# Windowed attention in two layers: when each stack of queries and keys is loaded, and which PSUM bank a late projection uses

## The chip, the cores and the metric

The kernel runs on one core of a Trainium2 chip. The metric is the device time of one execution in microseconds, as the median over runs. The core has five engines that run side by side, each through its own list of instructions in order: TensorE (PE; its weight loads are shown as PEld), VectorE (DVE), ScalarE (ACT), GpSimd (POOL) and SyncE (SP). SP, ACT and POOL can also issue DMAs; here most of them stand in SP's list. Semaphores make an instruction wait for others.

## The reference

The input is a sequence of 2048 tokens of 576 numbers. Four steps are added to it in turn: attention, a filter in the frequency domain, attention, the filter. Both attentions use the same weights, and so do both filters. The attention has 32 heads of 18 numbers, and a query sees itself and the 255 keys before it:

```
qkv = (layernorm(x) @ wqkv)  ->  q, k, v with H = 32 heads of Dh = 18
scores = einsum("bhqd,bhkd->bhqk", q, k) * Dh ** -0.5
mask = (idx[:, None] - idx[None, :] >= 0) & (idx[:, None] - idx[None, :] < 256)
p = softmax(where(mask, scores, -1e9))
x = x + einsum("bhqk,bhkd->bhqd", p, v) @ wo
x = x + irfft2(rfft2(layernorm(x)) * (w_r + 1j * w_i))
```

## The kernel before

One Python program writes all instructions, and the order in which it writes them is each engine's order. It builds two attention layers (`layer_a`), each followed by a filter layer (`layer_b`). The change is in `layer_a`, so it acts twice.

**Quads, chunks, blocks.** The 32 heads are worked on in 8 quads of four heads; a quad is two halves of partitions (hp) by two pairs. The 2048 tokens are 16 tiles of 128, and four tiles are a chunk. So a block, x = 16 n + i, is tile i of quad n, and there are 128 of them. (n, c) below is chunk c of quad n.

**Projections.** q and k of all heads are 1152 rows, computed as 9 groups of 128 rows by 4 chunks: `proj(i, c)`, 14 matmuls of 512 columns each into one PSUM bank (line 1112). The result is split into a rounded part, which ScalarE copies out (line 1124, CAST), and a remainder, which VectorE subtracts (line 1127). Then a DMA stores both to `qk_d` in DRAM (line 1129). The subtraction and the store are kept in the list `ended` and written when `remainders()` is called, so they come later in the engines' lists than the copy. Groups i = 0, 1 are projected first, groups 2 to 8 in pieces between the attention's own work; their 392 matmuls are the list `pj`. Staging tiles of groups 0 to 2 share room with the tiles of exponentials (tag "P", six of them).

**Stacks.** `stack_load(n, c)` (line 1135) brings one chunk of a quad's q and k from `qk_d` into one of two sets of tiles, `qs` and `ks`, quads n and n + 2 using the same set. It is twelve DMAs of 72 KB, six for q and then six for k; nearly all stand in SP's list. A chunk of quad n reads rows of two groups of projections: group n + 1 is the later one for n = 2 to 7.

**Scores, maxima, exponentials, sums.** For each block and head there is a score tile (`score_max`: matmul at line 1169, masked row maximum on VectorE at line 1171) and, ten blocks later (LEAD = 10), an exponent tile (`exps`: matmul at line 1206, exponential on ScalarE at line 1207, masks on GpSimd). Between the two, `m_rows(n, c)` transposes the maxima of a chunk on TensorE (line 1182), ScalarE copies them with the sign turned (line 1184), and four DMAs write them as a row of `qs` (line 1189, qs<-mt), from which the exponent matmul subtracts them. The exponent tile of block x reads tiles x to x + 2 of q, so it needs the row of the chunk that holds tile x + 2. `part(x, half)` adds the values weighted by the exponentials into the PSUM tile U (line 1226), and `norm` transposes the finished sums (line 1240), divides, and stores them (line 1251).

**Order.** `opening()` runs score tiles of blocks 0 to 9 with the first 70 matmuls of `pj`, which are projections (2,0) to (2,3) and (3,0). `bursts()` then covers blocks 0 to 117 in 158 bursts, k = 0 to 157. Each burst has three exponent tiles and three score tiles, that is three quarters of a block, and behind them a few matmuls of `pj`, or sums, or small tasks. `loads(x)` is called where a burst starts block x. How many matmuls of `pj` a burst gets follows from `ends`, the last burst in which each projection may run: (3,1) is spread over bursts 0 to 3, (3,2) over the next ones up to burst 8, and so on. Bursts listed in `values` (4, 7, 9, ...) have sums instead. Blocks 118 to 127 follow in a shorter loop.

**Near the end** SP's list also gets, from block 104 on, the output weights in two pieces (`out.room`, line 734), five constants (`out.const`, line 748, the first at block 107) and input tiles (`out.load_x`, line 759).

**PSUM.** It has eight banks. Tag "S" has three for score tiles, "E" three for exponent tiles (and, early, some projections and transposes), "pj" one for projections, and "U" one. In the opening every fourth score tile of a block uses "U"; from then on U holds the sums. Of each 32 rows of U only 19 are written by the sums, but the whole bank is copied and transposed, so it is set to zero once (line 1421).

Of the kernel before, what the change touches and what calls it, by code (L numbers as in the profile page):

```python
# [8 lines left out]
F32 = mybir.dt.float32  # L9
# [9 lines left out]
NT = 16  # L19
# [659 lines left out]
def k_steps():  # L679
    s = []  # L680
    for kt in range(4):
        s += [(kt, "h", kt), (kt, "h", 4 + kt)]
    for kt in range(4):
        s += [(kt, "l", kt)]
    s += [(4, "h", 8), (4, "l", 8)]
    return s
# [178 lines left out]
def layer_a(tc, ident, eps, bp, src, dst, wqk_d, wv_d, wo_d, dc_d, gc_d, dram, copy, wvs, second, spectral, share):  # L865

    nc = tc.nc
    V, A, T, P = nc.vector, nc.scalar, nc.tensor, nc.gpsimd
# [11 lines left out]
    def tokens(x, c):  # L880

        return x.rearrange("r (n p) -> r n p", n=NT)[:, :, 32 * c:32 * c + 32]
    if True:
        room = []

        def xT(k, c):

            xh, xl = room
            return xl[:, k - 4, c] if 4 <= k < 8 else xh[:, min(k, 4), c]
# [8 lines left out]
        def w_split(i):  # L898
            raw = wraws[i]
            h = bp.tile([128, 5, 128], F32R, tag="wqh", name=f"wqh{i}", bufs=2)  # L900
            l = bp.tile([128, 5, 128], F32R, tag="wql", name=f"wql{i}", bufs=2)
            wt[i] = (h, l)
            split_w(nc, raw, h, l, V if i == 2 else P)
            if i + 2 < 9:
                w_load(i + 2)
# [170 lines left out]
        with ExitStack() as c2:  # L1076
            wp = c2.enter_context(tc.tile_pool(name="a2", bufs=2))
            pp = Banks(tc, c2, "a2p", ("S", "pj"))
# [7 lines left out]
            for j in range(2):  # L1086
                q = wp.tile([128, 2, S], F32R, name=f"qs{j}", bufs=1)
                k = wp.tile([128, 2, S], F32R, name=f"ks{j}", bufs=1)
# [5 lines left out]
            def remainders():  # L1094
                while ended:
                    ended.pop(0)()

            def proj(i, c, bank=0):

                box = {}  # L1100
                ks = k_steps()
                cs = slice(c * 512, c * 512 + 512)

                def mm(s, k):
                    wk, p, xk = k
                    if s == 7 and c == 2 and 0 < i < 8:
                        w_split(i + 1)
                    if s == 0:
                        box["ps"] = pp.tile([128, 512], F32, tag="E" if bank else "pj", name=f"pj{i}_{c}", bufs=3 if bank else 1)
                    w = wt[i][0] if p == "h" else wt[i][1]  # L1110
                    x = tokens(xT(xk, slice(0, S)), c) if second else xT(xk, cs)
                    T.matmul(box["ps"].rearrange("r (n p) -> r n p", n=NT) if second else box["ps"], w[:, wk], x, start=s == 0, stop=s == len(ks) - 1)  # L1112
                    if s == len(ks) - 1:
                        if 4 * i + c < 12:

                            sg = wp.tile([128, 4, 384], F32, tag="P", name=f"sg{i}_{c}", bufs=6)
                            sg = sg.rearrange("r a b -> r (a b)")[:, 0:1024].rearrange("r (a t) -> r a t", a=2).bitcast(F32R)
                        else:
                            sg = wp.tile([128, 2, 512], F32R, tag="sg", name=f"sg{i}_{c}", bufs=2)
                        by, rest = box["ps"], sg  # L1120
                        if second:
                            by = by.rearrange("r (n p) -> r p n", n=NT)
                            rest = sg.rearrange("r a (p n) -> r a p n", n=NT)
                        A.copy(rest[:, 0], by)  # L1124

                        def remainder():
                            V.tensor_sub(rest[:, 1], by, rest[:, 0].bitcast(F32))  # L1127

                            (nc.scalar if i < 2 else nc.sync).dma_start(qk_d[:, 128 * i:128 * i + 128, cs].rearrange("a r t -> r a t").bitcast(F32), sg.bitcast(F32))
                        ended.append(remainder)  # L1130
                return [lambda s=s, k=k: mm(s, k) for s, k in enumerate(ks)]

            vts = {}
# [23 lines left out]
            def score_max(x, pair, hp):  # L1157
# [9 lines left out]
                four = x < LEAD and pair == hp == 1  # L1167
                ps = pp.tile([128, 512], F32, tag="U" if four else "S", name=f"S{x}_{pair}_{hp}", bufs=1 if four else 3)
                T.matmul(ps[:, 0:N], q[b:b + 63, pair, i * 128:i * 128 + 128], k[b:b + 63, pair, lo:hi], start=True, stop=True)  # L1169
# [47 lines left out]
            def part(x, half):  # L1217
# [6 lines left out]
                for h in range(4):  # L1224
                    if j >= 0:
                        T.matmul(U[32 * h:32 * h + 19, (q0 % 4) * 128:(q0 % 4) * 128 + 128 * (q1 - q0)], vts[n][:, j, h],  # L1226
                                 pt[n, j][:, h, (q0 - j) * 128:(q1 - j) * 128],
                                 start=j == max(e - 1, 0), stop=j == i or (i == e and j == i - 2), skip_group_check=True)
                if half and i % 4 == 3:
                    us[n, i // 4] = u = wp.tile([128, 512], F32, tag="us", name=f"us{n}_{i}", bufs=1)  # L1230
                    (V.tensor_copy if x >= MIX - 2 else A.copy)(u, U)  # L1231

# [29 lines left out]
                    stack_load(0, k // 2 - 1)  # L1262
            NX = NQ * NT
            LEAD = 10
            pj = [f for i in range(2, 9) for c in range(4) for f in proj(i, c, c % 2 if i == 2 else c == 0 and i == 3)]
            done, due = 0, []

            MIX = 118
# [1 line left out]
            def loads(t):  # L1270
                if t + LEAD in (0, 2):
                    stack_load(0, 2 + (t + LEAD) // 2)
                if t in (-4, 4, 8, 12):
                    stack_load(1, max(t, 0) // 4)
                n, c = divmod(t + 20, NT)
                if c % 4 == 0 and 1 < n < NQ:
                    stack_load(n, c // 4)
                if t + LEAD == 5:
                    v_load(0)
                if t + 12 in range(NT, NX, NT):  # L1280
                    v_load((t + 12) // NT)
# [28 lines left out]
            def bursts():  # L1310
# [2 lines left out]
                ss = [(x + LEAD, pair, 1 - hp) for x, pair, hp in es]  # L1313
                parts = [(x, half) for x in range(MIX - 2) for half in range(2) if x % NT]
                values = {(4 * x + 7) // 3 + 2 for x in range(0, MIX - 2, 2)}
                ends = [3] + [max(k - 1 for k in values if k - 1 <= 4 + 134 * (i + 1) // 22) for i in range(22)]
                unit = {k: i for i, end in enumerate(ends) for k in range(ends[i - 1] + 1 if i else 0, end + 1)}
                at = 70
                for k in range(-(-len(es) // 3)):
                    e, c = es[3 * k:3 * k + 3], ss[3 * k:3 * k + 3]  # L1320
# [28 lines left out]
                    n = 0  # L1349
                    if k in unit and k not in values:  # L1350
# [3 lines left out]
                        n = -(-rest // gaps)  # L1354
                        if gaps > 1 and any(f is norm for f, *a in tasks):
                            n = min(5, n + 1, rest - 2 * (gaps - 1))
# [60 lines left out]
            for f in opening():  # L1417
                f()
                done += 1
            U = pp.tile([128, 512], F32, tag="U", name="U", bufs=1)  # L1420
            V.memset(U, 0.0)
            for f in bursts():
                f()
                done += 1
# [18 lines left out]
            def bank(tag, name):  # L1443
                return pp.tile([128, 512], F32, tag=tag, name=name, bufs=1 if tag == "pj" else 3)

            out.early(0, [bank(k, f"ops0_{k}") for k in ("pj", "S")], slice(0, 4))
            tpz = [bank("E", f"tpz{k}") for k in range(3)] + [U]

# [16 lines left out]
            for u in range(3):  # L1465
                out.split_last(u, tp[:, 128 * u:128 * u + 128])
            out.turn(3, U, A)
            out.late(0)
# [50 lines left out]
```

## Time and profile before

| | us |
|---|---|
| median of 3 runs | 1366.31 (1366.28 to 1366.6) |
| the profiled execution | 1367.9 |
| its span, first to last instruction | 1366.2 |
| mean granted TensorE clock | 0.997 of full speed |
| attention bursts, first layer | from 127.6 |
| attention bursts, second layer | from 825.1 |

The profile of one execution is read through views. The page gives each engine's busy time. The waits name, for each line, what its engine waited for: total us, times, longest. The timeline lists instructions by engine: start, duration, engine, line, operation, output <- inputs, count, and in square brackets how long the engine stood idle and what released it. "SPq" is SP's own list of DMA issues; the duration there is that of issuing, not of the transfer. The windows give, for a stretch of time, its length and then the busy us of PE, PEld, DVE, ACT and POOL with the number of instructions, the granted TensorE clock, the share of the DMA engines, and GB/s. Bursts are found in the timeline by their first score tile. A PE that is busy need not be at its peak, and matmuls overlap, so the distance between starts tells more than durations.

### The profile page before, as it was taken

What the parts mean: (1) busy time and instruction counts of PE and PEld (TensorE: products, weight loads), DVE (VectorE), ACT (ScalarE), POOL (GpSimd) and SP (SyncE); (2) the same over time, 40 slices, a digit from 0 to 9 for tenths busy, and PEclk for the clock granted to TensorE, in tenths of its full rate; (3) what the DMA queues carried; (4) which work ended last, traced back from release to release, by engine and by line L of the source; (5) the groups of instructions that cost most, each with busy time, mean ns of one, the idle gap of its engine ahead of it and who ended that gap; (6) DMA issues with size and microseconds to landing.
All of it is one profiled execution on the core that took longest, in us unless ns stands there. A gap on an engine that the chain in (4) does not pass through costs nothing.

```text
span 1366.2 us, 33609 instructions
## 1 busy us (share of the span) xinstructions
PE 1335.8 (98%) x11351; PEld 997.2 (73%) x11351; DVE 900.5 (66%) x3060; ACT 780.0 (57%) x1966; POOL 644.0 (47%) x1154
## 2 busy tenths in 40 slices
PE   9999999999999999999999999999999999999998
PEld 8986666666665699975999965566666655898587
DVE  5418777877778376666663157777777785576745
ACT  5522777777778544542455316677777778464223
POOL 3257545555546533476221394455455458213721
PEclk9999999999999999999999999999999999999999
DMA  6756665655446457778773467555555555597875
GB/s 204 208 164 194 207 190 166 188 166 160 150 145 180 129 154 249 223 237 266 253 243 73 114 194 224 160 170 162 153 158 153 157 157 168 143 359 253 301 234 173
DMA packets 202425, 259.11 MB, mean 190 GB/s; under 512 B 104599, under 2 KB 109975, under 8 KB 201743
## 3 DMA queue, kind: packets, MB, share of 16 engines
q1 hardware_dynamic: 191551, 235.72, 57.0%
q10 hardware_dynamic: 7648, 14.96, 3.1%
q0 software_dynamic: 3056, 6.28, 1.8%
q8 instruction: 92, 1.51, 0.5%
q14 instruction: 78, 0.64, 0.2%
HBM read 156.11 MB, written 101.01 MB: 188 GB/s over the span
## 4 chain that ended last, share of the span: by engine, by line
PE 87%; DMA 4%; DVE 3%; ACT 2%; issue 2%; SPq 1%; POOL 0%; ACTq 0%; DVEq 0%; POOLq 0%
PE pj L1112 19%; PE S L1169 12%; PE U L1226 12%; PE vps L1005 8%; PE ops L800 7%; PE E L1206 6%; PE po L257 3%; PE pq L517 2%; PE tpo L1240 2%; PE pf L257 2%; PE p L496 2%; PE pi L591 2%; PE pz L295 2%; DMA ofree<-yd 1%; PE tpm L1182 1%
## 5 line engine op out<-in xcount | busy, mean ns | idle before, releaser
L1171 DVE CUSTOM_DVE_ANT_0 jk<-S,mask 128x384 bf16<-128x384 f32 (+2 forms) x1024 | 490.7, 529 | 113.5 <-PE E L1206 60.3
L1207 ACT ACTIVATE P<-E 128x384 f32<-128x384 f32 (+2 forms) x1024 | 409.1, 476 | 128.0 <-PE E L1206 99.2
L1209 POOL TENSOR_SCALAR_AFFINE_SELECT P<-P 128x512 f32<-128x512 f32 x256 | 162.6, 635 | 278.2 <-ACT P L1207 257.3
L1169 PE MATMUL S<-ks,qs 63*128 63x384 f32 (+2 forms) x1024 | 269.1, 371 | 1.0 <-DMA qs<-qk_d 0.4
L1206 PE MATMUL E<-qs,ks 64*128 64x384 f32 (+2 forms) x1024 | 222.4, 372 | 6.4 <-DMA qs<-mt 3.7
L1169 PEld LDWEIGHTS S<-ks,qs 63*128 63x128 f32 x1024 | 140.7, 185 | 105.4 <-DVE m L1171 72.4
L1226 PE MATMUL U<-P,vq 128*19 128x128 f32 (+1 forms) x3840 | 188.3, 329 | 0.6 <-DVE us L1231 0.2
L1112 PE MATMUL pj<-xh,wqh 128*128 128x512 f32 x360 | 156.2, 434 | 1.7 <-DVE sg L1127 1.3
L1226 PEld LDWEIGHTS U<-P,vq 128*19 128x19 f32 x3840 | 96.0, 98 | 77.7 <-issue 25.0
L1212 POOL TENSOR_SCALAR_AFFINE_SELECT P<-P 128x512 f32<-128x512 f32 x224 | 142.3, 635 | 0.0
L1206 PEld LDWEIGHTS E<-qs,ks 64*128 64x128 f32 x1024 | 113.7, 185 | 21.3 <-ACT P L1207 9.7
L1112 PE MATMUL pj<-xh,wql 128*128 128x512 f32 x360 | 124.4, 418 | 0.0
L1112 PE MATMUL pj<-xl,wqh 128*128 128x512 f32 x288 | 122.3, 425 | 0.0
L800 PE MATMUL ops<-oroom 128*128 128x290 f32 (+1 forms) x812 | 115.4, 298 | 0.4 <-DVE ofree L846 0.2
L800 PEld LDWEIGHTS ops<-oroom 128*128 128x128 f32 x812 | 110.2, 189 | 1.1 <-DVE ofree L823 0.7
L1112 PEld LDWEIGHTS pj<-xh,wqh 128*128 128x128 f32 x360 | 67.8, 188 | 32.5 <-issue 10.5
L1171 DVE DVE_READ_ACCUMULATOR2_ANT m<- 128x1 f32 x1024 | 85.3, 83 | 0.0
L1127 DVE TENSOR_TENSOR sg<-pj,sg 128x512 fp32r<-128x512 f32 x72 | 49.5, 687 | 52.5 <-ACT sg L1124 52.5
L1124 ACT CAST sg<-pj 128x512 fp32r<-128x512 f32 x72 | 42.2, 586 | 69.2 <-PE pj L1112 54.2
L1112 PEld LDWEIGHTS pj<-xh,wql 128*128 128x128 f32 x360 | 64.3, 189 | 20.3 <-issue 10.7
L1005 PE MATMUL vps<-wvh,xh 128*128 128x288 f32 x320 | 71.4, 304 | 0.0
L1112 PEld LDWEIGHTS pj<-xl,wqh 128*128 128x128 f32 x288 | 54.3, 189 | 18.3 <-issue 11.6
(599 smaller groups left out, 2257.5 us busy)
## 6 DMA issues: line engine op xcount, KB each, us to landing
qk_d<-sg SPq DMA_DIRECT2D x56, 512.0 KB
qs<-qk_d SPq DMA_DIRECT2D x384, 72.0 KB
ks<-qk_d SPq DMA_DIRECT2D x348, 72.0 KB
v_d<-vt SPq DMA_DIRECT2D x32, 304.0 KB
vq<-v_d SPq DMA_DIRECT2D x16, 608.0 KB
wt<-in_w SPq DMA_DIRECT2D x16, 580.0 KB
ofree<-x SPq DMA_DIRECT2D x16, 580.0 KB
x<-ofree SPq DMA_DIRECT2D x32, 290.0 KB
```

The source lines that it names most:

```text
L257: T.matmul(ps[:, c, 0:NF], tail[r] if si == 4 else hl_(si), dcs[b // 2][r, b % 2], start=mi == si == 0, stop=si == 4)
L800: self.nc.tensor.matmul(self.ps[u][n][:, 0:self.n], x, self.w[p][:, (2 * wk + n) * self.n:(2 * wk + n + 1) * self.n], start=first and i == ...
L1005: T.matmul(ps[:, n, 0:288], xT(xk, c), w[:, wk, n * 288:(n + 1) * 288], start=i == 0, stop=i == len(ks) - 1)
L1112: T.matmul(box["ps"].rearrange("r (n p) -> r n p", n=NT) if second else box["ps"], w[:, wk], x, start=s == 0, stop=s == len(ks) - 1)
L1127: V.tensor_sub(rest[:, 1], by, rest[:, 0].bitcast(F32))
L1169: T.matmul(ps[:, 0:N], q[b:b + 63, pair, i * 128:i * 128 + 128], k[b:b + 63, pair, lo:hi], start=True, stop=True)
L1171: V.tensor_tensor_reduce(out=jk[:, 0:N], in0=ps[:, 0:N], in1=mask[:, 384 - N:384], scale=1.0, scalar=-3e38, op0=ALU.add, op1=ALU.max, accu ...
L1206: T.matmul(ps[:, 0:nq], k[b:b + 64, pair, j * 128:j * 128 + 128], q[b:b + 64, pair, j * 128:j * 128 + nq], start=True, stop=True)
L1207: A.activation(p[:, hl_, 0:nq], ps[:, 0:nq], AF.Exp, scale=SC)
L1209: P.affine_select(out=p[:, :, 0:128], in_=p[:, :, 0:128], pattern=[[0, 4], [1, 128]], compare_op=ALU.is_ge, fill=0.0, base=0, channel_mult ...
L1212: P.affine_select(out=p[:, :, 256:384], in_=p[:, :, 256:384], pattern=[[0, 4], [-1, 128]], compare_op=ALU.is_gt, fill=0.0, base=0, channel ...
L1226: T.matmul(U[32 * h:32 * h + 19, (q0 % 4) * 128:(q0 % 4) * 128 + 128 * (q1 - q0)], vts[n][:, j, h], pt[n, j][:, h, (q0 - j) * 128:(q1 - j) ...
```

## The change

Five lines are edited.

- The loads of quads 2 to 7 are asked for four blocks later: (n, c) at block 16 n - 16 + 4 c instead of 16 n - 20 + 4 c. Quads 0 and 1 keep their own places.
- Projection (3,0), the last of the opening, uses the bank "pj" instead of one of the "E" banks.
- Projection (3,1), the first of the bursts, uses the tile U itself instead of the bank "pj"; it writes every row and column of it, and the line that sets U to zero is removed.
- `remainders()` is called once more between opening and bursts, so that the subtraction and store of (3,0) come ahead of burst 0's score tiles instead of behind them.
- (3,1) has to end with burst 2 instead of burst 3. Its 14 matmuls are then 5, 5, 4 in bursts 0 to 2 (before: 4, 4, 3, 3 in bursts 0 to 3), and those of (3,2) are 4, 4, 3, 3 in bursts 3, 5, 6, 8 (before: 5, 5, 4 in bursts 5, 6, 8). From burst 9 on nothing changes in that list.

```diff
@@ proj
                     if s == 0:
-                        box["ps"] = pp.tile([128, 512], F32, tag="E" if bank else "pj", name=f"pj{i}_{c}", bufs=3 if bank else 1)
+                        box["ps"] = U if bank == 2 else pp.tile([128, 512], F32, tag="E" if bank else "pj", name=f"pj{i}_{c}", bufs=3 if bank else 1)
@@ the list pj
-            pj = [f for i in range(2, 9) for c in range(4) for f in proj(i, c, c % 2 if i == 2 else c == 0 and i == 3)]
+            pj = [f for i in range(2, 9) for c in range(4) for f in proj(i, c, c % 2 if i == 2 else 2 if (i, c) == (3, 1) else 0)]
@@ loads
                 if t in (-4, 4, 8, 12):
                     stack_load(1, max(t, 0) // 4)
-                n, c = divmod(t + 20, NT)
+                n, c = divmod(t + 16, NT)
                 if c % 4 == 0 and 1 < n < NQ:
                     stack_load(n, c // 4)
@@ bursts
-                ends = [3] + [max(k - 1 for k in values if k - 1 <= 4 + 134 * (i + 1) // 22) for i in range(22)]
+                ends = [2] + [max(k - 1 for k in values if k - 1 <= 4 + 134 * (i + 1) // 22) for i in range(22)]
@@ after the opening
+            remainders()
             U = pp.tile([128, 512], F32, tag="U", name="U", bufs=1)
-            V.memset(U, 0.0)
```

## The prediction

> **What bounds the kernel now.** The page comes first. TensorE is busy for 98% of the span, so a change pays only where TensorE stands still, or where it does less work.
>
> ```profile
> span 1366.2 us, 33609 instructions
> PE 1335.8 (98%) x11351; PEld 997.2 (73%) x11351; DVE 900.5 (66%) x3060; ACT 780.0 (57%) x1966; POOL 644.0 (47%) x1154
> ```
>
> Next come TensorE's waits inside the attention of the first layer (125 to 520 us) and of the second (822 to 1170 us). Columns: total, times, longest.
>
> ```profile
> PE E L1206 <- ACT P L1207: 1.4, 3, 0.7
> PE E L1206 <- DMA qs<-mt: 1.2, 1, 1.2
> PE E L1206 <- DMA qs<-mt: 2.5, 1, 2.5
> ```
>
> Two kinds matter. In each layer one exponent tile waits for the row maxima that SP writes into the stack (qs<-mt), 1.2 and 2.5 us, and a few wait for an exponential to free a PSUM bank (the first row is the first layer's). Cut into bursts, with TensorE's busy time and granted clock, the places show. First layer: bursts 0, 1, 2, 3, 24, 25; second layer: bursts 0, 1, 24, 25.
>
> ```profile
> 127.61:130.57 2.96, 2.28 (x11) 1.26 (x10) 2.22 (x10) 1.85 (x4) 1.76 (x3) 1.00 0.41 131
> 130.57:133.29 2.72, 2.28 (x11) 1.26 (x10) 2.09 (x7) 1.36 (x3) 1.22 (x2) 1.00 0.89 220
> 133.29:134.92 1.63, 1.63 (x10) 0.96 (x10) 1.15 (x5) 1.12 (x3) 0.18 (x1) 1.00 1.02 331
> 134.92:136.71 1.79, 1.79 (x11) 1.12 (x10) 1.68 (x7) 1.42 (x5) 1.05 (x2) 1.00 0.84 219
> ...
> 177.36:181.67 4.31, 3.02 (x17) 1.77 (x14) 2.07 (x7) 2.16 (x5) 0.99 (x2) 1.00 0.45 134
> 181.67:183.18 1.51, 1.51 (x23) 0.85 (x22) 1.03 (x5) 0.99 (x3) 0.37 (x1) 1.00 0.56 153
> ...
> 825.10:827.92 2.82, 2.30 (x11) 1.26 (x10) 2.19 (x10) 1.85 (x4) 1.66 (x3) 1.00 0.79 217
> 827.92:830.67 2.75, 2.31 (x11) 1.26 (x11) 2.08 (x7) 1.36 (x3) 1.22 (x2) 1.00 1.19 254
> ...
> 874.33:880.30 5.97, 3.48 (x17) 1.91 (x14) 2.05 (x7) 2.11 (x5) 0.98 (x2) 0.90 0.41 123
> 880.30:882.80 2.50, 2.50 (x24) 1.33 (x23) 1.61 (x6) 1.25 (x3) 1.13 (x2) 0.55 0.69 223
> ```
>
> **Part 1: loads four blocks later.** From block 16 on, SP's list keeps its order; each place asks for the chunk that the place before it asked for. What differs is the ends: at block 12 one load of twelve DMAs instead of two, at block 108 one instead of none. SP's timeline at block 12, with the row transpose and the exponent tile that waited:
>
> ```profile
> 162.24 3.12 SPq L1144 DMA_DIRECT2D qs<-qk_d  x6
> ...
> 167.66 3.16 SPq L1144 DMA_DIRECT2D qs<-qk_d  x6
> 170.86 2.15 SPq L1144 DMA_DIRECT2D ks<-qk_d  x6
> ...
> 174.10 3.18 SPq L1189 DMA_DIRECT2D qs<-mt  x4
> ...
> 169.13 0.28 PE L1182 MATMUL tpm<-ident,m 128*16 128x128 f32 x1
> ...
> 179.01 1.03 PE L1206 MATMUL E<-qs,ks 64*128 64x384 f32 x3 [1.21 <-DMA qs<-mt]
> ```
>
> The transpose is done at 169.4, but its four DMAs stand behind 24 load DMAs and start at 174.10; the tile goes at 179.01 in a burst that began at 177.36. Without the second load SP is free at 167.6; a store and an output DMA follow, and the four start as soon as the copied maxima are there, near 170, four us earlier. That is more than either layer's wait, so it goes in full. Its price follows from burst 3, which has three projection matmuls and a row transpose and takes 1.79. One more matmul is 0.235 us, by the starts of two that follow each other:
>
> ```profile
> 129.78 0.40 PE L1112 MATMUL pj<-xl,wqh 128*128 128x512 f32 x1
> 130.02 0.39 PE L1112 MATMUL pj<-xh,wqh 128*128 128x512 f32 x1
> ```
>
> Burst 24 has five and the same transpose, so 2.26. It took 4.31 and 5.97, and burst 25 of the second layer took 2.50 against 1.51. That is 2.05 in the first layer and 3.71 + 0.99 = 4.70 in the second, **6.75 together**. Bounds: 5.05 if the half clock's 1.7 (below) comes back at some smaller hole, and 6.75.
>
> In the second layer the clock column falls to 0.90 and 0.55 after the hole of 2.5 us: 5.97 x 0.10 + 2.50 x 0.45 = 1.7 us of those 4.70. The first layer's hole of 1.2 us left it at 1.00. [...]
>
> What queues behind the moved load is the other side. Mid-run a load now has six blocks, eight bursts, before its first score tile. Loads (1,1) to (1,3) are asked six blocks ahead today, and in the two stretches above no score tile waits for qk_d; so I cost that at nothing, and the cover is those bursts, some 16 us for a load that takes 10 (162.24 to 167.6 on the queue at block 12, and its landing). The end has less cover, because bursts without projections are shorter. SP's timeline there, first layer, with burst 152's first score tile, two of SP's waits from 416 to 436 us, the same wait in the second layer, and the landing row (min/median/max) of such loads issued on GpSimd's queue:
>
> ```profile
> 416.73 2.12 SPq L1144 DMA_DIRECT2D qs<-qk_d  x6
> 418.89 2.35 SPq L1144 DMA_DIRECT2D ks<-qk_d  x6
> 421.33 0.84 SPq L734 DMA_DIRECT2D ofree<-in_wo  x2
> 422.73 3.08 SPq L1189 DMA_DIRECT2D qs<-mt  x4
> 425.91 0.94 SPq L1251 DMA_DIRECT2D o_d<-o  x2
> 427.99 2.33 SPq L748 DMA_DIRECT2D dc<-dcr  x2
> ...
> 434.74 0.44 PE L1169 MATMUL S<-ks,qs 63*128 63x384 f32 x1
> ...
> SPq L748 <- DMA ofree<-in_wo: 2.6, 2, 1.6
> SPq L1144 <- DMA qk_d<-sg: 2.1, 1, 2.1
> ...
> SPq L1144 <- DMA qk_d<-sg: 1.0, 1, 1.0
> ...
> DMA to landing us min/median/max: 3.1/3.8/6.2
> ```
>
> The constants (L748) wait for the output weights (L734) although they don't read them: two weight pieces, four rows and two outputs stand ahead, so the ninth DMA waits until the one eight before it has landed. Today (7,3) goes at 416.73, after 2.1 us of waiting for a store. Then (7,2) stands there, whose store is old, so everything to the weights moves 2.0 ahead. The new (7,3) comes after the first constant, and its first piece, eight behind the second weight piece, takes the second constant's place: 430.0 (430.32 less 0.33) less 2.0 = 428.0. Twelve at 0.375 (416.73 to 421.24) put the last at 432.1; landing takes 3.8, so 435.9. Burst 152's first score tile needs it at 434.74: **a new hole of 1.2 us** (0.5 with 3.1, 3.6 with 6.2). The four row DMAs of (7,1), due in the same burst, stand behind it and land about when it does. In the second layer the store is waited for 1.0 instead of 2.1, so the list moves ahead 1.1 less and the hole is 2.3, unless SP gets there sooner because the loads before it, too, have older stores, which would make it 1.3 or less. I take 1.8, halfway (0.6 with the fastest landing, 4.2 with the slowest). The two cost **3.0**, bounds 1.1 and 7.8; below nothing is excluded, since no transfer is removed there.
>
> **Part 2: projection (3,1) in the sums' bank, (3,0) in the projections' own.** Today (3,0) holds one of the three exponent banks until its remainder runs behind burst 0's score maxima. A burst without waiting is 1.63 with three projection matmuls, 1.87 with four, so bursts 0 and 1 lose 1.09 + 0.85 and 0.95 + 0.88 = 3.77. With three banks free both vanish, and the 14 matmuls of (3,1) go 5, 5, 4 instead of 4, 4, 3, 3. What is late next is on ScalarE and SP, first layer and then second:
>
> ```profile
> 128.99 1.11 SPq L1152 DMA_DIRECT2D vq<-v_d  x1
> 135.66 2.47 SPq L1129 DMA_DIRECT2D qk_d<-sg  x3
> ...
> 140.61 2.02 ACT L1207 ACTIVATE P<-E 128x384 f32<-128x384 f32 x5 [1.39 <-DMA qk_d<-sg]
> ...
> 837.39 0.87 ACT L1207 ACTIVATE P<-E 128x384 f32<-128x384 f32 x2 [0.78 <-DMA qk_d<-sg]
> ```
>
> Block 4's exponentials write into room from which projection (2,2) is still being stored; that store starts at 135.66, eight DMAs behind the value load, and has landed by 140.61. The edit moves none of this. So in burst 6 both kernels meet at the second and third exponent tile, and what stays is projection work done ahead: three matmuls of bursts 6 and 8, 0.7 us. In the second layer ScalarE waits 0.78 for that store instead of 1.39, so the kernels meet some 0.4 us sooner on the way and about 1.1 us stays. **Together 1.8**; bounds 0.7 (first layer alone) and 3.77.
>
> On VectorE the zeroing falls away and the remainder moves into its place:
>
> ```profile
> L1421 DVE MEMSET U<- x2: 485/485/485, 127.9 to 825.4; 128x512 f32 x2
> ...
> 130.37 0.69 DVE L1127 TENSOR_TENSOR sg<-pj,sg 128x512 fp32r<-128x512 f32 x1
> ```
>
> There the remainder also waits for ScalarE's copy, so burst 0's score maxima start some 0.8 us later (an estimate: that copy, not the zeroing, is what they then follow). Their banks are needed by burst 1, two us on: nothing on the path; without that cover 0.4 a layer. (3,1) must leave the sums' bank before burst 4 sums. Its remainder comes behind three score maxima of about half a us and takes 0.69, so it ends some 2.6 us into burst 3; burst 3 itself takes 2.03 with its four matmuls, and burst 4 issues six tiles ahead of its sums (0.7). Nothing, or 0.3 a layer if it slips. The store of (3,1) now goes ahead of four row DMAs in SP's list: 0.4 us in a queue whose rows are due a us later.
>
> **Sum.** The profiled execution took 1367.9, of which 1366.2 is the span: 1367.9 - 6.75 - 1.8 + 3.0 = 1362.4. The median of the runs shown is 1.6 lower, 1366.31, so it comes to **1360.8 us**.
>
> **Rivals.**
> - *Nothing is late at the end* (0.18). Landing like the fast loads, and ScalarE, which has exponentials in hand in these bursts, covers the rest: 1366.31 - 8.55 = 1357.8. Against it: 435.9 against 434.74.
> - *The end eats the gain* (0.08). With landings of 6.2 the two holes are 7.8: 1365.6.
> - *Slower by the late last load* (0.08). Place: bursts 152 of both layers. Holes of 3.6 and 4.2 us are longer than the 2.5 that halved the clock, which cost 1.7 each time, and the rows of (7,1) behind them may add 0.3 each (an estimate): 7.8 + 3.4 + 0.6 - 8.55 = +3.25, 1369.6. It decides from holes of 5.2 us together. For it: both constants wait for the weights; against: only the longest landing row gets there. By the trace a hole of 2.5 pays the 1.7; holes of 2.6 and 3.2 would then give 1366.31 - 8.55 + 5.8 + 3.4 = 1367.0. [...]
> - *The change doesn't do what it says* (0.06). The rows of (1,1) stay late behind the store and output that remain in front: only 1.8 - 3.0, so 1367.5. Against it: those two took a us at 173.
>
> **How the numbers follow.** The forecast has 0.60. The range, 1356.5 to 1365.6, runs from full use of the opening (1360.8 - 2.0) with half of the end hole hidden, and a us beyond the first rival, to the end that eats the gain; the forecast's own is 1358 to 1363.5. Changes under 0.2% (2.7 us) can't be told from none. Faster: 0.60 + 0.18 = 0.78. Same: 0.08 + 0.06 = 0.14. Slower: 0.08.
>
> **What would show it.** Right: no wait of an exponent tile for qs<-mt at burst 24, clock 1.00 there, bursts 0 and 1 near 2.1 us with five projection matmuls each, ScalarE still waiting for qk_d<-sg at block 4, and a new wait of a score tile for qs or ks<-qk_d at burst 152 of some 1 to 2 us. Wrong: score tiles waiting for loads in mid-run, the sums of burst 4 waiting for a remainder, or a clock under 1.00 at the end of an attention.

## The result

The changed kernel takes **1372.91 us** (median of 5 runs, 1369.51 to 1375.61), the kernel before beside it 1366.31 (1364.25 to 1366.6): a ratio of 1.0048, 95% interval 1.0031 to 1.0066. It is slower by 6.6 us, where 5.5 less was forecast, and above the range. The profiled execution took 1370.44; its span and first lines:

```profile
span 1368.7 us, 33664 instructions
PE 1340.6 (98%) x11351; PEld 998.6 (73%) x11351; DVE 899.7 (66%) x3058; ACT 778.8 (57%) x1966; POOL 643.9 (47%) x1154
```

TensorE's work is the same 11351 matmuls and takes 4.8 us longer than the 1335.8 of before. To find where, the attention is cut at the starts of bursts: bursts 0 to 8, 9 to 18 and 19 to 27 and the drain of the first layer, then bursts 19 to 27 and the drain of the second. The drain is the stretch from the start of burst 145 to that of block 120 in the loop behind the last burst; it has no projections. A hole is a stretch in which TensorE stands idle. Columns of the windows view: from:to, length, busy time (and instructions) of PE, PEld, DVE, ACT and POOL, granted clock, DMA share, GB/s. Before:

```profile
127.62:147.44 19.82, 18.57 (x133) 10.91 (x133) 14.84 (x59) 13.69 (x33) 10.62 (x16) 1.00 0.77 242
147.44:168.04 20.60, 20.60 (x222) 12.93 (x222) 16.23 (x65) 15.75 (x40) 10.80 (x18) 1.00 0.60 180
168.04:187.76 19.72, 18.43 (x164) 11.39 (x164) 14.66 (x56) 12.21 (x32) 7.80 (x13) 1.00 0.56 176
423.23:448.43 25.20, 24.88 (x263) 13.54 (x259) 19.35 (x80) 21.60 (x57) 19.02 (x28) 1.00 0.62 184
864.99:887.22 22.23, 19.74 (x166) 11.80 (x165) 14.75 (x56) 12.15 (x32) 7.76 (x13) 0.92 0.52 166
1123.96:1149.00 25.04, 24.71 (x261) 13.72 (x257) 19.16 (x80) 21.59 (x57) 19.02 (x28) 1.00 0.67 193
```

The same stretches of the changed kernel:

```profile
127.47:145.90 18.43, 18.20 (x135) 10.95 (x134) 14.12 (x58) 13.23 (x32) 10.55 (x16) 1.00 0.77 252
145.90:167.56 21.66, 21.57 (x221) 13.51 (x220) 16.32 (x65) 15.88 (x40) 10.79 (x18) 1.00 0.60 176
167.56:185.16 17.60, 17.60 (x165) 11.01 (x164) 14.55 (x56) 11.89 (x32) 7.80 (x13) 1.00 0.51 159
421.04:448.86 27.82, 26.25 (x262) 14.05 (x258) 19.48 (x80) 21.80 (x57) 18.99 (x28) 0.94 0.59 176
866.57:884.27 17.70, 17.70 (x165) 10.95 (x165) 14.56 (x56) 11.89 (x32) 7.75 (x13) 1.00 0.54 171
1121.21:1150.38 29.17, 26.14 (x261) 13.87 (x257) 19.48 (x80) 21.86 (x57) 19.03 (x28) 0.94 0.58 176
```

Read row against row. Burst 24's hole is gone as forecast: 2.12 + 4.53 = 6.65 us. The drains lose as much: 2.62 + 4.13 = 6.75. The opening of the first layer gains 1.39 in bursts 0 to 8 and returns 1.06 of it in bursts 9 to 18. In TensorE's timeline the drains' losses begin at burst 152 in both layers, as waits for the last load (shown as dc<-dcr, the constant that shares its semaphore) and for the rows behind it:

```profile
433.69 0.41 PE L1169 MATMUL S<-ks,qs 63*128 63x384 f32 x1 [1.25 <-DMA dc<-dcr]
434.27 0.98 PE L1206 MATMUL E<-qs,ks 64*128 64x384 f32 x3 [0.16 <-DMA qs<-mt]
...
1134.30 0.41 PE L1169 MATMUL S<-ks,qs 63*128 63x384 f32 x1 [1.65 <-DMA dc<-dcr]
1135.72 1.12 PE L1206 MATMUL E<-qs,ks 64*128 64x384 f32 x3 [1.01 <-DMA qs<-mt]
```

The holes are 1.41 and 2.66 us, and after each of them the granted clock is 0.50 for 3.41 us, from 436.54 and from 1136.28. The windows view of the changed kernel around the first, two rows that hold the hole (its longer part runs from 432.44 to 433.69) and the one behind them:

```profile
429.72:433.13 3.41, 2.73 (x36) 1.29 (x34) 3.17 (x13) 3.12 (x8) 2.60 (x4) 1.00 0.70 195
433.13:436.54 3.41, 2.68 (x19) 1.51 (x21) 1.79 (x8) 1.95 (x5) 1.52 (x3) 1.00 0.59 124
436.54:439.95 3.41, 3.41 (x28) 1.76 (x26) 1.60 (x6) 1.55 (x4) 1.22 (x2) 0.50 0.50 190
```

SP's timeline of the changed kernel before the first hole, and two rows of SP's waits from 412 to 437 us, show what the last load waits for:

```profile
416.58 0.84 SPq L734 DMA_DIRECT2D ofree<-in_wo  x2
417.84 2.76 SPq L1189 DMA_DIRECT2D qs<-mt  x4
...
423.10 0.33 SPq L748 DMA_DIRECT2D dc<-dcr  x1
425.25 2.11 SPq L1144 DMA_DIRECT2D qs<-qk_d  x6
...
430.39 2.66 SPq L1189 DMA_DIRECT2D qs<-mt  x4
```

```profile
SPq L1144 <- DMA ofree<-in_wo: 1.8, 1, 1.8
SPq L748 <- DMA ofree<-in_wo: 0.7, 1, 0.7
```

The output weights go out at 416.58, 4.75 us earlier than before (421.33); the first constant and the last load, (7,3), still wait until they have landed, and the rows of (7,1) stand behind the load.

Over the bursts the two profiles come out within 0.4 us of each other. The 2.5 between the two executions lies outside them, where the changed kernel has two half-clock stretches of 3.41 us (at 812.0 and 1266.0) and the one before has one (at 643.6). One profile each therefore can't tell why the medians differ by 6.6.

### The profile page after: what moved, and what is told of

Read it like the earlier page. It is cut to its first block, busy times and chain, and to the rows that moved or that the text cites. A ratio compares the mean times of both kernels' runs of the same rounds, so it can differ in the third digit from the quotient of the medians.

```text
span 1368.7 us, 33664 instructions
## 1 busy us (share of the span) xinstructions
PE 1340.6 (98%) x11351; PEld 998.6 (73%) x11351; DVE 899.7 (66%) x3058; ACT 778.8 (57%) x1966; POOL 643.9 (47%) x1154
## 4 chain that ended last, share of the span: by engine, by line
PE 87%; DMA 5%; DVE 3%; issue 1%; ACT 1%; SPq 1%; POOL 0%; DVEq 0%; ACTq 0%; POOLq 0%
PE pj L1112 19%; PE S L1169 13%; PE U L1226 12%; PE vps L1005 9%; PE ops L800 7%; PE E L1206 6%; PE po L257 4%; PE pq L517 2%; PE tpo L1240 2%; PE p L496 2%; PE pf L257 2%; PE pi L591 2%; PE pz L295 1%; DMA yd<-ye 1%; DMA ofree<-yd 1%
## 5 line engine op out<-in xcount | busy, mean ns | idle before, releaser
L1112 PE MATMUL pj<-xh,wqh 128*128 128x512 f32 x350 | 152.1, 435 | 0.9 <-DVE sg L1127 0.6
L1112 PE MATMUL pj<-xh,wql 128*128 128x512 f32 x350 | 120.9, 419 | 0.0
L1112 PE MATMUL pj<-xl,wqh 128*128 128x512 f32 x280 | 119.4, 426 | 0.0
L1112 PEld LDWEIGHTS pj<-xh,wqh 128*128 128x128 f32 x350 | 66.1, 189 | 30.9 <-issue 10.3
```

## The experiments

Theory A: the later loads cost in the drains, by holes and the half clock behind them, more than they save at burst 24. Theory B: the part with the bank and the remainder costs it. The medians, each beside runs of the kernel before on the same chip:

| run | us | kernel before | ratio (95%) |
|---|---|---|---|
| loads alone (e1) | 1366.12 | 1362.20 | 1.0032 (1.0014 to 1.0051) |
| bank part alone (e2) | 1364.17 | 1362.20 | 1.0012 (0.9997 to 1.0027) |
| loads spread (e3) | 1373.95 | 1362.20 | 1.0080 (1.0057 to 1.0102) |
| weights behind the last load (e4) | 1384.08 | 1362.20 | 1.0159 (1.0132 to 1.0186) |
| last two loads ahead of the weights (e6) | 1369.64 | 1364.70 | 1.0043 (1.0024 to 1.0062) |
| one load moved, block 12 to 14 (e8) | 1364.19 | 1364.70 | 0.9993 (0.9978 to 1.0009) |
| weights on another queue (e9) | 1370.45 | 1364.70 | 1.0045 (1.0029 to 1.0061) |
| changed kernel again (e10) | 1369.41 | 1364.70 | 1.0031 (1.0017 to 1.0045) |
| only the last load late (e12) | 1364.64 | 1362.54 | 1.0006 (0.9994 to 1.0017) |
| old bank, double load at block 24 (e13) | 1361.82 | 1362.54 | 0.9992 (0.9980 to 1.0004) |
| new bank, double load at block 24 (e14) | 1360.86 | 1362.54 | 0.9988 (0.9972 to 1.0005) |
| old bank, double load at block 56 (e15) | 1360.42 | 1362.51 | 0.9984 (0.9972 to 0.9996) |
| new bank, double load at block 56 (e16) | 1361.09 | 1362.51 | 0.9988 (0.9975 to 1.0000) |
| new bank, double load at block 72 (e17) | 1362.81 | 1362.51 | 0.9996 (0.9984 to 1.0008) |

**Which part.** e1, on the kernel before, and e2, on the changed kernel:

```
-                n, c = divmod(t + 20, NT)
+                n, c = divmod(t + 16, NT)
```

```
-                n, c = divmod(t + 16, NT)
+                n, c = divmod(t + 20, NT)
```

> The kernel before with the loads of quads 2 to 7 asked for four rounds later, and nothing else of the change. Theory A (the later loads pay at the drain what they save at burst 24, and the colder stretches behind them cost the rest): the hole at burst 24 goes, holes on the copy dc<-dcr and a half clock come at burst 152 to 154 in both layers, and the time is near the changed kernel's, 1369 to 1375 us. Theory B (the part with the bank and the remainder costs it): 1366 us or less.

> The changed kernel with the loads of quads 2 to 7 asked for as before, so that only the bank, the remainder and the first end are changed. Theory A: no hole on the last load at burst 152, the hole at burst 24 as before, and at most the 1.4 us of the opening gained: 1364 to 1366.5 us. Theory B: 1368 to 1373 us.

The loads alone make it slower by 3.9 us, the bank part by 2.0 with an interval that includes zero; together that is the change. e1's profile, which is the slowest of its twelve runs (1375.09), has the drains of the changed kernel (28.08 and 30.24 us), e2's those of the kernel before (24.90 and 24.91). A is borne out for the larger part, and B is not excluded for the rest.

**Why the last load is late.** e3 spreads the 24 loads evenly, with the last at block 104; e4 asks for the weights behind the last load; e6 moves the last two loads ahead of the weights. All on the changed kernel:

```
-                n, c = divmod(t + 16, NT)
-                if c % 4 == 0 and 1 < n < NQ:
-                    stack_load(n, c // 4)
+                for j in range(24):
+                    if t == 16 + round(88 * j / 23):
+                        stack_load(2 + j // 4, j % 4)
```

```
-                if t == OB - 16:
+                if t == OB - 12:
                     out.room()
-                if 0 <= t - (OB - 10) < 10 and t % 2 == 0:
-                    out.split((t - (OB - 10)) // 2)
+                if 0 <= t - (OB - 6) < 10 and t % 2 == 0:
+                    out.split((t - (OB - 6)) // 2)
```

```
-                if c % 4 == 0 and 1 < n < NQ:
+                if c % 4 == 0 and 1 < n < NQ and t < 104:
                     stack_load(n, c // 4)
+                if t in (102, 104):
+                    stack_load(7, t // 2 - 49)
```

> The changed kernel with the 24 loads of quads 2 to 7 spread evenly over blocks 16 to 104 (one in nearly every fourth block, the last at 104 in place of 108). Theory A: neither the double load at block 12 nor the late last load; the gain at burst 24 (6.75 us) is kept and the 6.6 us lost in the drains is not: 1358 to 1362 us. Theory B, or a loss by cold stretches elsewhere: 1366 us or more.

> The changed kernel with the output projection's weights asked for at block 108, behind the last load instead of four blocks ahead of it, and their splits four blocks later. Theory A with the queue as the reason: the last load lands in time, the hole at burst 152 goes in both layers, and the time is 1359 to 1364 us, if the weights' splits do not become late in their turn. If the last load is late for its own place and not for the weights ahead of it, the hole stays and the time stays at 1369 to 1375 us.

> The changed kernel with the last two loads (chunks 2 and 3 of quad 7) asked for at blocks 102 and 104 instead of 104 and 108, so that both stand ahead of the output weights; all else as changed. Theory A (the last load behind the weights, and the half clock that its hole brings, costs what the change loses): no hole on dc<-dcr at burst 152 in either layer, no half clock there, burst 24 still without its hole, and 4 to 7 us less than the changed kernel run beside it. Rival (the bank part or the colder stretches between the attentions cost it): within 2 us of the changed kernel.

e3 missed: its drains are as before, but it loses 4.0 and 2.3 us in the first layer at bursts 50 and 66, where an exponent tile waits 2.0 and 1.8 us for rows that SP now issues behind a load. Against e15's profile (below) it also loses 1.7 and 2.2 at the same bursts of the second layer, and 4.0 at bursts 13 and 14 of the first. e4 says little: the input tiles now overwrite part of the weights before they are split. In its first layer the score tile no longer waits for the load, but an exponent tile of the same burst waits 4.4 us for rows. e6 missed as well, within noise of the changed kernel. The hole at burst 152 went as expected, but TensorE's timeline has one eleven bursts earlier (and one of 1.5 us at the same place of the second layer), on rows behind the two loads:

```profile
416.09 0.41 PE L1206 MATMUL E<-qs,ks 64*128 64x384 f32 x1 [2.41 <-DMA qs<-mt]
```

So theory A in its first form falls: the order of weights and loads isn't the cause by itself. e9 takes the weights off SP's queue, on the changed kernel:

```
-            self.nc.sync.dma_start(self.raw[:, a * X:b * X], self.wo_d[:, a * X:b * X])
+            self.nc.gpsimd.dma_start(self.raw[:, a * X:b * X], self.wo_d[:, a * X:b * X])
```

> The changed kernel with the two loads of the output weights issued from GpSimd's queue instead of SP's, at the same place. If the last load is late because the weights' slow landings hold two of the eight places of SP's queue: the hole on dc<-dcr at burst 152 shrinks or goes in both layers, 2 to 6 us less than the changed kernel beside it. If the DMA engines themselves are the limit: the hole stays, within 1.5 us of it; GpSimd's own issuing work could cost up to 2 us more.

> The changed kernel once more, unaltered, beside the others. Theory A: the holes of 1.2 to 1.7 us on dc<-dcr at burst 152 are there again in both layers, each with a half clock behind it, and the time is 4 to 8 us above the kernel before. If the half clocks at the drains fell there by chance in the first profile: at least one is missing here and the time is within 3 us of the kernel before.

No gain. GpSimd issues the weights at 412.90, in the middle of the load (7,2), where SP issued them behind it at 416.58. In e9's TensorE timeline the hole comes six bursts earlier and is larger; SP's timeline shows four row DMAs that take 6.58 us to issue where they took 2.76; and the list of DMA issues (last column: us to landing) has the larger weight piece at 10.3 us:

```profile
425.45 0.44 PE L1169 MATMUL S<-ks,qs 63*128 63x384 f32 x2 [2.73 <-DMA ks<-qk_d]
```

```profile
418.06 6.58 SPq L1189 DMA_DIRECT2D qs<-mt  x4
```

```profile
ofree<-in_wo POOLq DMA_DIRECT2D x1, 864.0 KB, 10.3
```

So the queue alone isn't the cause either: SP's rows wait 5.4 us in all for landings of the load (7,2) ahead of them, which share the 16 DMA engines with the weights: from 411 to 427 us queue q1, which holds SP's list, takes 31.1% of the engines' time and q0, GpSimd's, 29.1%. e10 confirms the drains, with 1.9 and 5.3 us lost against 24.9. Its first-layer hole is longer than that of the first profile, yet the clock stays whole behind it. The windows after the timeline row are the two drains, and then two that hold the first layer's hole, laid out in steps of 3.413 us back from its half-clock stretch (1133.74 to 1140.57; below):

```profile
434.95 0.41 PE L1169 MATMUL S<-ks,qs 63*128 63x384 f32 x1 [2.23 <-DMA ks<-qk_d]
```

```profile
421.30:448.15 26.85, 24.27 (x262) 13.34 (x258) 19.32 (x80) 21.73 (x57) 19.06 (x28) 1.00 0.61 179
1119.06:1149.30 30.24, 27.50 (x261) 14.62 (x257) 19.50 (x80) 21.95 (x57) 19.08 (x28) 0.89 0.52 156
430.59:434.01 3.42, 2.13 (x31) 0.99 (x31) 2.74 (x12) 3.12 (x8) 2.85 (x4) 1.00 0.62 143
434.01:437.42 3.41, 2.47 (x21) 1.54 (x21) 1.82 (x7) 1.70 (x5) 0.93 (x2) 1.00 0.66 161
```

e12 delays the last load alone, on the kernel before:

```
-                n, c = divmod(t + 20, NT)
-                if c % 4 == 0 and 1 < n < NQ:
+                n, c = divmod(t + 20 - 4 * (t == 108), NT)
+                if c % 4 == 0 and 1 < n < NQ and t != 104:
                     stack_load(n, c // 4)
```

> The kernel before with one load moved: the last chunk of quad 7 is asked for at block 108 instead of 104; all else as before. If the late last load is what the change loses at its end: a hole at burst 150 to 153 in both layers, a half clock behind at least one of them, and 4 to 8 us more than the kernel before run beside it. If the drain's loss needs the whole queue four blocks later: within 2 us of the kernel before.

Its drains (windows view, both layers) are whole, although SP's timeline has the load only 0.6 us earlier than the changed kernel (425.25). The last row is burst 152's first score tile:

```profile
422.54:447.45 24.91, 24.58 (x262) 13.46 (x258) 19.16 (x80) 21.60 (x57) 19.01 (x28) 1.00 0.56 162
1122.52:1147.42 24.90, 24.57 (x261) 13.46 (x258) 19.16 (x80) 21.61 (x57) 19.04 (x28) 1.00 0.56 162
```

```profile
424.65 2.18 SPq L1144 DMA_DIRECT2D qs<-qk_d  x6
...
433.80 0.43 PE L1169 MATMUL S<-ks,qs 63*128 63x384 f32 x1
```

What differs more is TensorE: it starts burst 145 at 422.54 here and at 421.04 in the changed kernel. At burst 152 it arrives at 433.80, without a wait, where in the changed kernel it stood ready at 432.44 (433.69 less the idle 1.25). These 1.4 us and the load's 0.6 cover that wait. **The load lands when the queue gets to it; how much of a hole that makes depends on how early TensorE arrives.** This is read from one profile of each kernel; no run delays TensorE alone. e6, e9 and e12 fit a drain that lacks room for two loads and the weights within eight blocks, which is argued, not shown.

**What the hole at burst 24 is worth.** e8 moves one load, e13 lets the double load fall on block 24, where the rows due next belong to a quad's first block and are used two blocks later, and e15 on block 56. All on the kernel before; e14, e16 and e17 (block 72) are the same on the changed kernel.

```
+                if c % 4 == 0 and 1 < n < NQ and t > 12:
                     stack_load(n, c // 4)
+                if t == 14:
+                    stack_load(2, 0)
```

```
+                if t in (16, 20, 24):
+                    stack_load(2, t // 4 - 4)
                 n, c = divmod(t + 20, NT)
+                if c % 4 == 0 and 1 < n < NQ and t > 20:
```

```
+                n, c = divmod(t + 16, NT)
+                if c % 4 == 0 and 1 < n < NQ and t <= 56:
+                    stack_load(n, c // 4)
                 n, c = divmod(t + 20, NT)
+                if c % 4 == 0 and 1 < n < NQ and t >= 56:
```

> The kernel before with one load moved: the first chunk of quad 2 is asked for at block 14 instead of together with the last chunk of quad 1 at block 12; all later loads stay where they were. Theory A: the double load alone makes the hole at burst 24, so that hole goes (5 us, 6.7 where a half clock followed it) and nothing comes at the drain: 3 to 7 us less than the kernel before. Rival (the hole at burst 24 comes from the queue's load in general): the hole stays, within 1.5 us of the kernel before.

> The kernel before with the first three loads of quad 2 asked for at blocks 16, 20 and 24 instead of 12, 16 and 20, and all others as before, so that the two loads that fall on one block do so at block 24 instead of block 12, ahead of rows that are used at a quad's first block (in the traces so far these rows land 7 to 8 us ahead of their use, those behind block 12 after it). Theory C (the double load costs only where rows are due close behind it): no hole at burst 24 in either layer, none of 0.5 us at bursts 40 to 46, the ends as in the kernel before: 4 to 7 us less than it. Rival (the queue as a whole is late, and a hole taken away at one place comes back at the next): the hole comes back within the next 30 bursts, within 1.5 us of the kernel before.

> The kernel before with the loads of quads 2 to 4 up to block 56 asked for four blocks later, as in the change, and from block 56 on as before, so that two loads fall on block 56 instead of block 12. If the profiles' gain at burst 24 (1.2 us in the first layer, some 4 in the second, as means over the profiles) is there in runs without a profile too: 4 to 6 us less than the kernel before, with no hole of 0.5 us behind bursts 74 to 110. If the double load costs as much wherever it is put, or the hole at burst 24 is smaller in runs without a profile: within 2 us of it.

e8 changes nothing: block 14 is no better, the second layer's hole stays at 1.5 us, and the first layer has a new hole of 2.0 at burst 34. In e13 the hole at burst 24 is gone, but bursts 48 to 74 of the first layer take 1.6 us more than in e15. The backlog may have reached later rows; no wait over 0.2 us there shows it. e15 has neither; its windows view (bursts 19 to 27 and the drain, first layer, then second):

```profile
167.46:185.07 17.61, 17.61 (x164) 10.97 (x163) 14.55 (x56) 11.91 (x32) 7.82 (x13) 1.00 0.44 148
420.61:445.50 24.89, 24.56 (x261) 13.45 (x257) 19.16 (x80) 21.59 (x57) 19.07 (x28) 1.00 0.60 180
861.78:879.49 17.71, 17.71 (x166) 10.95 (x165) 14.57 (x56) 11.90 (x32) 7.82 (x13) 1.00 0.51 166
1116.16:1141.07 24.91, 24.59 (x262) 13.46 (x258) 19.15 (x80) 21.75 (x57) 19.09 (x28) 1.00 0.65 191
```

It gains at burst 24 in both layers and loses nothing in the drains, and yet it is only 2.1 us (0.5 to 3.8) faster than the kernel before, not 6.65. Three more profiles of that kernel, unaltered, tell much of the reason:

> The kernel before, once more, with a profile of another execution. If the hole at burst 24 is a property of the kernel: again a wait of 0.9 to 2.6 us on qs<-mt in both layers. [...]

> The kernel before, a third profile. If the hole at burst 24 differs from one execution to the next (so that the gain of the runs with the double load at block 56, 2.1 us, is a mean over executions with and without it): bursts 19 to 27 take 17.6 to 19.8 us in the first layer and 17.7 to 22.3 in the second, and these move with the time of the execution, so that one at or below the median of 1362.5 us shows under 3 us of it in all. If the hole is always there in full: 5 us or more in all whatever the execution's time.

> The kernel before, a fourth profile, with the same two expectations as the third.

Bursts 19 to 27 of both layers, in the windows view, of the executions that took 1365.89, 1363.55 and 1361.96 us:

```profile
167.65:185.91 18.26, 18.26 (x166) 11.40 (x165) 14.63 (x56) 12.15 (x32) 7.78 (x13) 1.00 0.54 177
864.17:885.28 21.11, 19.83 (x166) 11.88 (x165) 14.74 (x56) 12.15 (x32) 7.76 (x13) 0.92 0.53 171
```

```profile
168.26:187.23 18.97, 18.34 (x165) 11.38 (x165) 14.62 (x56) 12.15 (x32) 7.82 (x13) 1.00 0.55 174
861.89:882.90 21.01, 19.79 (x164) 11.96 (x163) 14.75 (x56) 12.15 (x32) 7.79 (x13) 0.92 0.54 174
```

```profile
166.59:185.48 18.89, 18.35 (x166) 11.41 (x165) 14.64 (x56) 12.15 (x32) 7.79 (x13) 1.00 0.53 170
862.22:881.43 19.21, 18.47 (x166) 11.37 (x165) 14.65 (x56) 12.15 (x32) 7.76 (x13) 1.00 0.53 171
```

Against 17.60 and 17.70 without the hole, the four executions lose 6.65, 4.1, 4.7 and 2.8 us there; e12, which has the same loads up to that place, loses 6.1. The hole's length and the clock behind it (0.92 over the second layer's stretch in three of the four, 1.00 in the last) vary from one execution to the next, and the profile that the prediction was made from has the largest of the four, in the slowest of the four.

**What the bank part is worth.**

> The changed kernel (bank, remainder and first end as changed) with the loads of the run before this one: the first three loads of quad 2 at blocks 16, 20 and 24, all others as in the kernel before. Against the run with the old bank: if the bank part pays, 1 to 2 us less; if its gain in the opening comes back as a hole at bursts 13 and 14, where the rows stand behind the loads of quad 1, within 1 us of it or up to 3 us more. Against the kernel before by theory C: 3 to 8 us less.

> The changed kernel (bank, remainder and first end as changed) with the loads as in the run before this one: four blocks later up to block 56, as before the change from there on. If the ends alone make the changed kernel slow: 5 to 9 us less than the changed kernel's median of 1369.4 on its chip, so that it is at the kernel before or up to 5 us below it. If the loads of quads 2 to 4 cost it too: 2 us or less below the changed kernel. Against the run before this one: the bank part's worth, from the profiles 0.6 us the wrong way.

> The changed kernel with the loads four blocks later up to block 72 and as before from there on. As the run with block 56 where the double load is hidden there too (rows 7 to 8 us ahead of their use at the quad's first block, 3 to 5 behind it): within 1.5 us of that run. If the backlog of a double load reaches rows with less room: holes of 0.3 to 1 us at bursts 122 to 126 and 1 to 3 us more.

e14 against e13 is 1.0 us less and e16 against e15 0.7 more: nothing that can be told from zero, nor is e2's 2.0. e16 shows how the opening's gain returns (windows: bursts 0 and 9 on, first layer; timeline: the tile that waits):

```profile
127.53:145.83 18.30, 18.21 (x134) 10.94 (x134) 14.13 (x58) 13.24 (x32) 10.25 (x16) 1.00 0.77 257
145.83:168.67 22.84, 21.61 (x223) 13.52 (x222) 16.33 (x65) 15.99 (x40) 10.84 (x18) 1.00 0.55 168
```

```profile
155.83 0.78 PE L1206 MATMUL E<-qs,ks 64*128 64x384 f32 x2 [1.23 <-DMA qs<-mt]
```

The tile waits for rows that SP issues behind a load, a value load and a weight. In the first profiles these four DMAs begin at nearly the same time, before and after, though TensorE is 1.5 us ahead by then:

```profile
148.80 2.45 SPq L1189 DMA_DIRECT2D qs<-mt  x4
```

```profile
148.37 2.46 SPq L1189 DMA_DIRECT2D qs<-mt  x4
```

More than the gain can return. In e2's profile an exponent tile waits 1.2 us for these rows at burst 13 of the first layer. At burst 6 of the second ScalarE waits 2.5 us for the projection's store, and TensorE 1.5 behind it. The granted clock falls in both stretches, to means of 0.93 and 0.92, each what one stretch of 3.41 us at 0.50 would make (24.24 x 0.07 and 21.18 x 0.08 are both 1.7 us; windows: bursts 9 to 18 of the first layer, 0 to 8 of the second):

```profile
146.55:170.79 24.24, 23.06 (x221) 14.59 (x220) 16.36 (x65) 15.99 (x40) 10.79 (x18) 0.93 0.51 159
824.89:846.07 21.18, 19.70 (x135) 11.42 (x134) 14.18 (x58) 13.24 (x32) 10.55 (x16) 0.92 0.79 232
```

Bursts 0 to 18 of both layers together take 79.6 to 81.8 us in the nine profiles with the old bank (mean 80.5) and 79.7 to 85.0 in the ten with the new one (mean 81.4): no gain is left there.

e16 is also the test of the ends: it differs from the changed kernel only in the loads from block 56 on, which it asks for as before the change, and stands at 0.9988 of the kernel before where e10 stands at 1.0031. Some 5.9 us, give or take 2.6, thus come from the late loads of the second half, and e16's drains say where:

```profile
422.01:446.90 24.89, 24.56 (x261) 13.44 (x258) 19.15 (x80) 21.60 (x57) 19.07 (x28) 1.00 0.60 179
1114.96:1139.85 24.89, 24.57 (x263) 13.56 (x259) 19.16 (x80) 21.57 (x57) 19.09 (x28) 1.00 0.62 182
```

e17, with the double load at block 72, is not told from e16; its drains are 25.94 and 25.84 us.

The fastest version is e15, 0.16% ahead of the kernel before. That is less than the 0.2% that the prediction takes as the least that can be told from none, though its interval leaves out 1.

## Why the prediction was wrong

- **Part 1, burst 24: right in mechanism, too large.** The wait is gone and the clock is 1.00. 6.75 was forecast, 6.65 came between the two profiles, but the four profiles of the kernel before give 4.6 as a mean, and moving the double load without a price elsewhere gave 2.1 in runs (0.5 to 3.8). The step that failed is the price from one execution, which was then set against the median by one common difference of 1.6 us. Why the runs give less than the mean of four profiles is open; the interval ends short of it.
- **Loads in mid-run at nothing: right.** No score tile waits for a load ahead of burst 152.
- **The end: the step that failed most.** "I take 1.8, halfway" and 1.2 stood for the holes: 3.0; they came out at 1.41 and 2.66, 4.1 in all, inside the bounds. (These mix two cases: 0.6 is 1.3 less 0.7, but 4.2 is 1.8 and 2.4, where 2.3 and 2.4 make 4.7.) But the cost was 6.75 in that profile, because the clock fell to 0.50 behind the holes (27.82 x 0.06 and 29.17 x 0.06, some 1.7 us each); against 24.9 in each layer it is 7.2 there, 7.3 in e10 and 8.5 in e1, 7.7 as a mean. The prediction let that begin only with holes of 2.5 us and left it to a rival that "decides from holes of 5.2 us together". A hole of 1.41 was enough there. That 1.2 came so near to 1.41 in the first layer is luck. The sum shifted SP's list by its own reasons alone and set the landing against TensorE's old time, 434.74, although it counts gains of 2.75 us in that layer ahead of it. TensorE was ready at 432.44, 2.3 earlier, but the load came earlier too, at 425.25 instead of 428.0, and the two errors nearly cancel.
- **The opening: wrong in what is late next.** 0.7 and 1.1 were forecast behind ScalarE's wait at block 4. Bursts 0 to 8 gained 1.4 and 0.1. ScalarE's wait was taken as a place where the kernels meet; with TensorE ahead it became a hole of 1.5 us with a clock of 0.92 over the stretch in e2. The next thing late was not looked for past it: the row DMAs at burst 13, which keep SP's time. In runs the part is worth nothing measurable.
- **The sum by what was measured**: -2.1 (runs) or -4.6 (profiles) at burst 24, 0 for the opening, +7.7 for the drains: 3.1 to 5.6 slower, against 6.6 (4.2 to 9.0) and, in e10, 4.2 (2.3 to 6.1). By the ratios of the runs alone, from the kernel before over e15 and e16 to e10: -2.2 for the load moved at burst 24, +0.6 for the bank, +5.9 for the late loads of the second half, together 4.2.
- **The rivals**: the one with the half clock in both layers (1369.6) had the right mechanism and the wrong point from which it decides.

## What to carry to other kernels

When several stages stand against one DMA queue that has little room, a gain upstream on TensorE moves its arrival and can end as a wait there (here 1.39 us gained in bursts 0 to 8, 1.06 returned in bursts 9 to 18); look for the next place where a transfer keeps the queue's time, and price the gain up to there. Here the loads up to block 56 could be put off by four blocks (e15: bursts 19 to 27 in 17.61 and 17.71 us, both drains in 24.9), those behind it not as well (changed kernel: drains of 27.82 and 29.17), and a double load has to go somewhere: it was cheap in mid-run at block 56. A hole read in one profile is one draw; take the same stretch from several executions before it becomes a term of a sum, and add the half clock's price, here 1.7 us, to any hole of a microsecond or more as a chance (here 22 of 31, see below).

## What was not expected of the hardware

In the 19 profiles, the half-clock stretches ahead of the kernel's end last 3.41 us or twice that, once in e4 three times that. In the first profile of the changed kernel they start at 436.54, 812.01, 1136.28 and 1265.98, the later ones 110, 205 and 243 times 3.413 us after the first (829.44 / 243 for the last); in that of the kernel before they start at 643.63 and 879.15, 69 times 3.413 apart. Whether a hole brings one isn't set by its length alone: 1.41 us did in the changed kernel's profile, 2.23 didn't in e10. Nor does it decide that a hole lies across a boundary of steps of 3.413 us counted from a half-clock stretch of the same execution, for both of these do. Counted over the 19 profiles, with gaps less than 1.5 us apart taken as one hole, the attention between burst 0 and block 120 has 31 holes of 1 us or more. A half clock starts in or within 3.5 us behind 22 of them: at all nine of 2.29 us or more, and at 13 of the 22 shorter ones. TensorE need not stand still for the 3.41 us ahead of such a stretch: ahead of the first, from 433.13 to 436.54, it is busy for 2.68. A busy share that decides was not found either: e10's stretches of the same length with 2.13 and 2.47 us busy kept the full clock. What sets the half clock is not shown by these runs.

The kernel before spread from 1358.0 to 1369.3 us over the chips used here. The hole at burst 24 and the half clock behind it, which change from one execution to the next, are one part of this spread that the profiles show.
